# Ten instead of five first columns of q and k in fp32, the second five rounded on VectorE

## The chip, the cores and the metric

The kernel runs on one core of a Trainium2 chip. The metric is the device time of one execution in microseconds, the median of several runs. Profiles come from single executions of the same program; their "span" goes from the first to the last instruction and is a few microseconds shorter than the device time.

## The reference, cut to what matters

Four batches of channel attention are followed by a mixture of eight low-rank adapters with the two best chosen by gate.

```
B, N, C = (4, 6400, 256)
qn = q / (np.linalg.norm(q, axis=1, keepdims=True) + 1e-06)
kn = k / (np.linalg.norm(k, axis=1, keepdims=True) + 1e-06)
s = kn.transpose(0, 2, 1) @ qn / tau
a = np.exp(s - s.max(-1, keepdims=True))
a /= a.sum(-1, keepdims=True) + 1e-09
x = (v @ a).reshape(B * N, C)
...
z = x[mask] @ A[e]
delta[mask] += w[mask, k, None] * (z @ B[e])
...
return (x + delta).astype(np.float32)
```

The norms and the product of k and q run over the 6400 positions, so all of a batch's q and k has to be read before its attention matrix `a` (256 x 256) exists; only then can its v be worked on.

## The kernel before, in words

**Tiles.** The 6400 positions of a batch lie on 128 partitions with 50 "columns" each, and one column is 128 positions of 256 channels. A row of a column in DRAM is 1 KB of fp32. q and k of a batch are held in two halves of 25 columns (`QK`), v in five tiles of ten columns. In SBUF they are bf16: the loads issued by GpSimd (line 710, in the profile POOL) round fp32 to bf16 on the way. There are four `qk` tiles, so the load of a later batch's half waits until every reader of an earlier half is done.

**The work on q and k.** For each column `do_G` (line 753 for k with q, 757 for k with k, 761 for q with q) adds to an accumulator in PSUM. The diagonal of k with k and of q with q gives the norms. To spare TensorE, the table `OFF` takes some groups of five columns out of lines 757 and 761; for these, ScalarE squares the group (`do_sq`, line 776) and VectorE adds the squares up (`do_add`, line 783). The first group goes to a sum tile `ssq`, later groups through one single buffer `sq`, so square and add take turns. At the end of a batch `do_red` (789, 792) halves the sum down to 256 numbers, `do_n2p` (798) adds over the partitions on TensorE, `do_n2` (817) takes the diagonal, with ScalarE's copy of the accumulator (805), and reciprocal roots, exponentials and a transpose make the attention matrix. In batch 0 the groups taken out are 0, 1, 2, 3, 4, 6, 7 of k and 0, 2, 4, 5, 9 of q.

**The work on v.** Each tile of v is transposed on TensorE (`T`, 940), copied out of PSUM, multiplied with the attention and adapter weights (`ZL`, 964), gated on VectorE, and multiplied out (`Y`, 1067 and 1072); ScalarE and VectorE copy the outputs to the buffer `y` (920, 922), and SyncE stores them (1083).

**The order.** A planner in Python (`Plan.run`) works out a fixed order of instructions on every engine before the kernel is built, from estimated times. Some stores are held until a certain load has landed (`HOLD`).

**The opening.** Loads through GpSimd can round, loads through SyncE and ScalarE can't. The first five columns of q and k of batch 0 go the second way, as fp32, q issued by SyncE and k by ScalarE, ahead of everything else (`first_ahead`). They land in the first slot of the not yet used output buffer `y`. ScalarE rounds them into the `qk` tiles (`do_cast`, line 925), k first and then q, since the plan expects them so. `PARTS` cuts the rest of the first half: columns 5 to 16 and 17 to 24 are two more loads for each of q and k, issued by GpSimd. The adapter weights, 264 KB in three small loads, are issued by SyncE and ScalarE right behind the early columns and land in slot 1 of `y`; VectorE rounds them in `do_wts` (678, 681, 683). The last 16 partitions of columns 40 to 49 of batch 0 come by an indirect load (706).

The planner's steps and times are the same in both kernels.

Of the kernel before, what the change touches and what calls it, by code (L numbers as in the profile page):

```python
# [32 lines left out]
class Clock:  # L33


    WINDOW, FIRST, LOW, HIGH = 3.413, 0.31, 0.5, 0.8
# [249 lines left out]
def make_plan(B, order, ahead):  # L286
# [6 lines left out]
    for kind, b, i in order:  # L293
        if kind == "v":
# [3 lines left out]
            continue  # L298
        for c, n in PARTS.get((b, i), QK[i:i + 1]):
            for h in "qk":  # L300
# [3 lines left out]
    for h in "qk":  # L304
        p.add(("cast", h), {"ACT": 1.2}, [("load", h, 0, 0) + PARTS[0, 0][0]], 0)
    for b in range(B):

        for i, (c0, n) in enumerate(QK):
            for c in range(c0, c0 + n):
                deps = [k for k in p.steps if k[0] == "load" and k[2:4] == (b, i) and k[1] != "v"  # L310
                        and k[4] <= c < k[4] + k[5]]
                if (b, c) < (0, PARTS[0, 0][0][1]):
                    deps = [("cast", k[1]) for k in deps]
# [32 lines left out]
        if b == 0:  # L346
            p.add(("wts",), {"DVE": 2.12}, [("load", "k", 0, len(QK) - 1) + PARTS[0, len(QK) - 1][1]], -200)

# [118 lines left out]
        ('k', 2, 0), (2, 2): ('v', 1, 3), (2, 3): ('v', 2, 2), (3, 3): ('v', 2, 2)}  # L467

PARTS = {(0, 0): ((0, 5), (5, 12), (17, 8)), (0, 1): ((25, 17), (42, 8)), (3, 1): ((25, 17), (42, 8))}
REST, REST_AT, FULL, SIDE = (0, 1), 40, 112, 5  # L470
SLOTS = ((0, 4), (32, 34), (4, 6), (8, 12), (40, 42), (28, 32), (60, 62), (64, 68), (96, 98), (92, 96), (124, 126))
NO_WARM = {0, 1, 2, 3, 4, 5, 6, 7, 8, 9, 10, 11, 12, 24, 25, 26, 27, 28, 29}
# [105 lines left out]
def kernel(  # L578
# [11 lines left out]
    nc = tc.nc  # L590
# [15 lines left out]
    q_v = q.rearrange("b (p c) d -> b p c d", p=P)  # L606
    k_v = k.rearrange("b (p c) d -> b p c d", p=P)
# [10 lines left out]
    W = {}  # L618
# [3 lines left out]
    def y_slot(n):  # L622
        return Y[:, n * PC:(n + 1) * PC, :]
# [34 lines left out]
    held = {}  # L658

    def sb(s, kind, name, shape, dtype, part=""):  # L660

        if (kind, name, part) not in held:
            held[kind, name, part] = sbuf.tile(
                shape, dtype, tag=f"{kind}{at[kind, name]}{part}", name=f"{kind}{part}")
        return held[kind, name, part]
# [19 lines left out]
    def do_load(s, what, b, i, c, n):  # L685
        if what == "v":
            t, src = VS[:, at["v", (b, c // PC)] * PC:, :], v_v
        elif c + b:
            t = sb(s, "qk", (what, b, i), [P, max(n for _, n in QK), C], BF16)[:, c - QK[i][0]:, :]
            src = {"q": q_v, "k": k_v}[what]  # L690
        else:
            sb(s, "qk", (what, b, i), [P, max(n for _, n in QK), C], BF16)
            lo = "qk".index(what) * n
            W[what] = y_slot(0)[:, lo:lo + n, :]

            early.append((nc.sync if what == "q" else nc.scalar).dma_start(
                W[what], {"q": q_v, "k": k_v}[what][b, :, 0:n, :]))
            return
        r = P
        if what != "v" and (b, i) == REST:  # L700
            if c + n == NC:
                t, n, c, r = held["qk", (what, b, i), ""][:, REST_AT - QK[i][0]:, :], NC - REST_AT, REST_AT, FULL
            else:
                n = REST_AT - c
                for w in "qk" if what == "q" else "":
                    nc.gpsimd.indirect_dma_start(
                        W["side" + w].rearrange("p c d -> p (c d)"), None,
                        {"q": q, "k": k}[w].rearrange("b n d -> (b n d)").rearrange("(m w) -> m w", w=SIDE * C),
                        bass.IndirectOffsetOnAxis(ap=W["slots"], axis=0), bounds_check=B * N // SIDE - 1, oob_is_err=False)
        loaded[s.key] = nc.gpsimd.dma_start(t[0:r, 0:n, :], src[b, 0:r, c:c + n, :]).ins.name  # L710
# [211 lines left out]
            nc.vector.tensor_copy(out, in_)  # L922

    def do_cast(s, what):
        nc.scalar.copy(held["qk", (what, 0, 0), ""][:, 0:PARTS[0, 0][0][1], :], W[what])

    def do_warm(s, n):
        if n in NO_WARM:
# [149 lines left out]
    def do_store(s, b, i, c, n):  # L1078
# [3 lines left out]
        for rows in SHARES if (b, i) in SPLIT else (P,):  # L1082
            r = nc.sync.dma_start(out_v[b, p:p + rows, lo:lo + n, :], Y[p:p + rows, at_y:at_y + n, :])
            if (b, i) in HOLD and not p:
# [4 lines left out]


    do = dict(load=do_load, wts=do_wts, sq=do_sq, add=do_add, red=do_red, n2p=do_n2p, warm=do_warm, cast=do_cast, G=do_G, accs=do_accs, n2=do_n2, rsqrt=do_rsqrt, rq_ps=do_rq_ps, s=do_s,
              exp=do_exp, recip=do_recip, aT_ps=do_aT_ps, aT=do_aT, waA_ps=do_waA_ps, waA=do_waA,
              a=do_a, ZL=do_ZL, ZLe=do_ZLe, T=do_T, Te=do_Te, log=do_log, loge=do_loge, Z=do_Z, Ze=do_Ze, gzT=do_gzT,
# [56 lines left out]
```

## Time and profile before

| What | Value |
| --- | --- |
| median of 3 runs | 250.67 us (250.59 to 250.84) |
| the profiled execution | 250.69 us |
| its span | 245.0 us |
| TensorE busy | 213.6 us, 87% |
| VectorE busy | 185.4 us, 76% |
| ScalarE busy | 169.0 us, 69% |
| read and written in HBM | 79.90 MB and 26.21 MB, 433 GB/s over the span |
| GpSimd's loads (q0) | 38.67 MB as written in bf16 |
| hardware queues (q1 of SyncE, q10 of ScalarE) | 25.56 MB and 0.79 MB |

How to read it. PE is TensorE, PEld its weight loads, DVE VectorE, ACT ScalarE, POOL GpSimd, SP SyncE. A group's line has the source line, engine, operation, and "output<-input". In the timeline the first two numbers are the start and the length in microseconds, and brackets at the end hold the engine's idle time before the instruction and what ended it. A line of the waits says who waited for whom, microseconds in total, how often, and the longest. The chain of waits is followed back from the last instruction to what released it. A line of the DMA queues gives packets, megabytes and the packets' time as a share of sixteen DMA engines. q0's bytes are counted as written, bf16, so that it reads twice as many.

The opening in the before kernel, by view of the DMA issues: the early q was issued at 0.00 us and landed 4.9 us later, the early k at 0.12 with 5.9; GpSimd's first loads of q and k (12 columns) were issued at 1.44 and 2.09 and landed after 8.9 and 11.9 us.

### The profile page before, as it was taken

How to read it: one execution, taken by the hardware profiler on the slowest of the kernel's cores; microseconds unless marked ns; L12 is line 12 of the kernel's file. 1: busy time of each engine (PE TensorE's matmuls, PEld its weight loads, DVE VectorE, ACT ScalarE, POOL GpSimd, SP SyncE). 2: the span in 40 equal slices, each digit the busy share in tenths (PEclk: the TensorE clock that was granted, in tenths of full speed). 3: DMA queues.
4: the chain of work that ended last, by engine and by line, in shares of the span. 5: the costliest groups of instructions: out<-in, count | busy, mean ns of one | idle time of the engine just before them, and what ended most of it. 6: DMA issues, size and time to landing. Idle time of an engine off the chain costs nothing.

```text
span 245.0 us, 5349 instructions
## 1 busy us (share of the span) xinstructions
PE 213.6 (87%) x2203; PEld 178.1 (73%) x2024; DVE 185.4 (76%) x514; ACT 169.0 (69%) x316; POOL 27.6 (11%) x61
## 2 busy tenths in 40 slices
PE   0379099499898999999987999999999999999996
PEld 0257067158666998879877787999876799999985
DVE  1045578467869789999977889998989578788681
ACT  2944442274766769898796677999453599988885
POOL 7800200300020003000201003110000000000000
PEclk9999859769999999999999999999999999999999
DMA  8999999999999999999999999999999999999999
GB/s 276 214 214 217 210 231 205 214 222 214 215 216 218 220 209 217 221 215 206 243 290 258 318 295 206 214 221 223 306 213 301 352 381 283 309 407 438 422 416 417
DMA packets 8906, 65.36 MB, mean 267 GB/s; under 512 B 1201, under 2 KB 1585, under 8 KB 5170
## 3 DMA queue, kind: packets, MB, share of 16 engines
q0 software_dynamic: 5872, 38.67, 75.8%
q1 hardware_dynamic: 2674, 25.56, 25.2%
q10 hardware_dynamic: 336, 0.79, 0.9%
q8 instruction: 16, 0.26, 0.4%
q14 instruction: 8, 0.07, 0.1%
HBM read 79.90 MB, written 26.21 MB: 433 GB/s over the span
## 4 chain that ended last, share of the span: by engine, by line
DMA 39%; PE 37%; DVE 9%; issue 8%; ACT 6%; POOL 1%; POOLq 0%; ACTq 0%
DMA v<-in_v_dram 27%; PE Y_ps L1067 11%; DMA qk<-in_q_dram 7%; PE Y_ps L1072 5%; PE ZL_ps L964 5%; PE T_ps L940 5%; DMA qk<-in_k_dram 5%; DVE ssq L783 4%; PE acc L753 4%; PE gzT_ps L1054 3%; ACT sq L776 3%; DVE gz L1042 2%; PE acc L757 2%; ACT y L920 1%; POOL qk L710 1%
## 5 line engine op out<-in xcount | busy, mean ns | idle before, releaser
L753 PE MATMUL acc<-qk 128*128 128x256 bf16 (+1 forms) x400 | 77.5, 290 | 18.1 <-DMA qk<-in_k_dram 9.6
L783 DVE TENSOR_TENSOR ssq<-ssq,sq 128x1280 f32<-128x1280 f32 (+1 forms) x35 | 52.0, 1487 | 19.5 <-ACT sq L776 19.5
L753 PEld LDWEIGHTS <-qk 128*128 128x128 bf16 (+1 forms) x400 | 39.9, 105 | 31.0 <-DMA qk<-in_k_dram 10.3
L920 ACT COPY y<-Y_ps 128x512 f32<-128x512 f32 x87 | 50.7, 594 | 15.3 <-PE Y_ps L1072 12.8
L776 ACT ACTIVATE sq<-qk 128x1280 f32<-128x1280 bf16 (+1 forms) x35 | 44.8, 1280 | 23.2 <-DVE ssq L783 20.7
L1067 PE MATMUL Y_ps<-a_bf,vT 128*128 128x256 bf16 x400 | 60.0, 272 | 0.2 <-DVE zl L922 0.2
L1067 PEld LDWEIGHTS <-vT 128*128 128x128 bf16 x400 | 38.3, 98 | 5.2 <-issue 0.5
L1072 PE MATMUL Y_ps<-ball,gzT 128*128 128x256 bf16 x200 | 38.2, 273 | 0.0
L1042 DVE TENSOR_TENSOR gz<-zl,gatega 128x256 bf16<-128x256 f32 x95 | 35.4, 443 | 0.5
L757 PE MATMUL acc<-qk 128*128 128x128 bf16 (+1 forms) x170 | 32.6, 225 | 0.0
L940 PE MATMUL T_ps<-ident,v 128*128 128x128 f32 x200 | 25.8, 274 | 4.5 <-DMA v<-in_v_dram 4.2
L761 PE MATMUL acc<-qk 128*128 128x128 bf16 (+1 forms) x200 | 28.7, 227 | 0.0
L964 PE MATMUL ZL_ps<-waA_sb,vT 128*128 128x136 bf16 x380 | 26.3, 223 | 0.4 <-ACT y L920 0.3
L920 ACT COPY vT<-T_ps 128x512 f32<-128x512 f32 (+1 forms) x47 | 22.7, 546 | 4.6 <-PE T_ps L940 4.4
L940 PEld LDWEIGHTS T_ps<-ident,v 128*128 128x128 f32 x200 | 21.7, 141 | 5.8 <-issue 4.4
L964 PEld LDWEIGHTS <-vT 128*128 128x128 bf16 x380 | 23.8, 98 | 1.4 <-issue 0.4
L761 PEld LDWEIGHTS <-qk 128*128 128x128 bf16 (+1 forms) x200 | 19.1, 102 | 4.9
L920 ACT COPY zl<-ZL_ps 128x408 f32<-128x408 f32 (+1 forms) x50 | 19.9, 457 | 3.4 <-PE ZL_ps L964 3.4
L1054 PE MATMUL gzT_ps<-ident,gz 128*128 128x128 f32 x100 | 19.7, 280 | 2.0 <-DVE gz L1042 1.9
L1072 PEld LDWEIGHTS <-gzT 128*128 128x128 bf16 x200 | 19.5, 98 | 2.4 <-DVE gzT L922 0.2
L710 POOL DMA_DIRECT2D qk<-in_q_dram x11 | 6.2, 560 | 104.4 <-ACT y L920 40.2
L922 DVE COPY zl<-ZL_ps 128x272 f32<-128x272 f32 (+1 forms) x26 | 12.7, 497 | 6.9 <-PE ZL_ps L964 6.6
(91 smaller groups left out, 220.0 us busy)
## 6 DMA issues: line engine op xcount, KB each, us to landing
out_dram<-y SPq DMA_DIRECT2D x10, 1280.0 KB, 12.1
out_dram<-y SPq DMA_DIRECT2D x4, 2560.0 KB, 17.4
v<-in_v_dram POOLq DMA_DIRECT2D x14, 640.0 KB, 27.6
qk<-in_q_dram POOLq DMA_DIRECT2D x5, 1600.0 KB, 16.4
qk<-in_k_dram POOLq DMA_DIRECT2D x5, 1600.0 KB, 23.4
v<-in_v_dram POOLq DMA_DIRECT2D x3, 1280.0 KB, 28.6
out_dram<-y SPq DMA_DIRECT2D x3, 512.0 KB, 5.8
qk<-in_q_dram POOLq DMA_DIRECT2D x1, 1088.0 KB, 19.9
```

The lines of the kernel that those rows point to most:

```text
L753: nc.tensor.matmul(acc[ic][:, 0:256], kt[0:r, j, ic::CC], qt[0:r, j, :], start=c == 0, stop=False, skip_group_check=True)
L757: nc.tensor.matmul(acc[ic][:, 256:384], kt[0:r, j, ic::CC], kt[0:r, j, ic::CC], start=False, stop=False, skip_group_check=True)
L761: nc.tensor.matmul(acc[ic][:, 384:512], qt[0:r, j, ic * P:(ic + 1) * P], qt[0:r, j, ic * P:(ic + 1) * P], start=False, stop=c == NC - 1, s ...
L776: nc.scalar.activation(out[0:r, 0:n, :], t[0:r, j:j + n, :], ACT.Square)
L783: nc.vector.tensor_tensor(out=t, in0=t, in1=held["sq", (w, b, g), ""][0:r, 0:n, :], op=OP.add)
L920: nc.scalar.copy(out, in_)
L940: nc.tensor.matmul(ps[:, j, :], vt[:, c + j, :].bitcast(FP32), W["ident32"], is_transpose=True, start=(j == 0), stop=(j == n - 1))
L964: nc.tensor.matmul(ps[:, j, :], vT_of(b, i, c + j)[:, :, ic], st[b]["waA"][:, ic, :], start=(j == 0 and ic == 0), stop=(j == n - 1 and ic ...
L1042: nc.vector.tensor_tensor(out=pairs[:, h].rearrange("p c (e r) -> p c e r", e=E), in0=z[:, 2 * h:2 * h + 2, :].rearrange("p c (e r) -> p c ...
L1054: nc.tensor.matmul(ps[:, j, :], pairs[:, j * P:(j + 1) * P], W["ident32"], is_transpose=True, start=(j == 0), stop=(j == n // 2 - 1))
L1067: nc.tensor.matmul(ps[:, j, :], vT_of(b, i, c + j)[:, :, ic], st[b]["a"][:, ic, :], start=(j == 0 and ic == 0), stop=False, skip_group_che ...
L1072: nc.tensor.matmul(ps[:, j, :], pair[:, :, j], W["B"], start=False, stop=(j == 1), skip_group_check=True)
```

## The change

The early loads bring ten columns instead of five, in slot 0 of `y` for q and slot 3 for k. GpSimd's loads that the plan calls columns 5 to 16 now bring 10 to 16. ScalarE rounds the first five columns as before; VectorE rounds the next five, k and then q, right after ScalarE's instruction in the program.

```
+FIRST = 10
...
-            lo = "qk".index(what) * n
-            W[what] = y_slot(0)[:, lo:lo + n, :]
+            W[what] = y_slot(3 * "qk".index(what))
 
             early.append((nc.sync if what == "q" else nc.scalar).dma_start(
-                W[what], {"q": q_v, "k": k_v}[what][b, :, 0:n, :]))
+                W[what], {"q": q_v, "k": k_v}[what][b, :, 0:FIRST, :]))
             return
         r = P
+        if what != "v" and b == 0 and c < FIRST:
+            t, n, c = t[:, FIRST - c:, :], c + n - FIRST, FIRST
...
     def do_cast(s, what):
-        nc.scalar.copy(held["qk", (what, 0, 0), ""][:, 0:PARTS[0, 0][0][1], :], W[what])
+        n = PARTS[0, 0][0][1]
+        nc.scalar.copy(held["qk", (what, 0, 0), ""][:, 0:n, :], W[what][:, 0:n, :])
+        nc.vector.tensor_copy(held["qk", (what, 0, 0), ""][:, n:FIRST, :], W[what][:, n:FIRST, :])
```

## The prediction

> **What bounds the kernel now.** I read the page first, then the waits of TensorE, then the chain of waits in order of time, and last the timeline of the opening.
>
> ```profile
> span 245.0 us, 5349 instructions
> ...
> DMA  8999999999999999999999999999999999999999
> ...
> q0 software_dynamic: 5872, 38.67, 75.8%
> q1 hardware_dynamic: 2674, 25.56, 25.2%
> ```
>
> The DMA engines are busy in every slice but the first: the two large queues alone fill 101% of sixteen engines. So the time is that of the stream of bytes, plus a start and a tail. The median of the runs is 250.67 us; the profiled one took 250.69, so 5.7 us lie outside the span of 245.0 and everything below is reckoned inside the span.
>
> ```profile
> PE T_ps L940 <- DMA v<-in_v_dram: 4.2, 4, 2.5
> PE gzT_ps L1054 <- DVE gz L1042: 1.3, 2, 1.2
> ```
>
> These are TensorE's own waits between 50 and 135 us. It waits four times for v, the last time 2.49 us until 130.14. The chain of waits shows the same corner:
>
> ```profile
> 26.92 16.40 DMA qk<-in_q_dram
> ...
> 92.88 37.13 DMA v<-in_v_dram x2
> 130.14 2.38 PE T_ps L940 x20
> ```
>
> Before 130 us the stream of loads leads; from 130.14 the chain runs through TensorE, which is busy over 9.4 us in every 10 up to 240. So the end moves as the landing at 130.0 moves, unless something makes TensorE more than about 4.2 us late before that (its waits for v are its slack).
>
> The change acts in the opening, whose timeline on ScalarE is a serial chain:
>
> ```profile
> 6.03 2.42 ACT L925 CAST qk<-y 128x1280 bf16<-128x1280 f32 x2 [2.00 <-DMA y<-in_k_dram]
> 8.35 2.42 ACT L776 ACTIVATE ssq<-qk 128x1280 f32<-128x1280 bf16 x2
> 10.68 1.25 ACT L776 ACTIVATE sq<-qk 128x1280 f32<-128x1280 bf16 x1
> ...
> 14.04 1.27 ACT L776 ACTIVATE sq<-qk 128x1280 f32<-128x1280 bf16 x1 [2.11 <-DMA qk<-in_k_dram]
> ```
>
> After the two casts come two squares, then square and add take turns (one sq buffer): one turn is 2.83 us (14.04, 16.87, 19.70 ...). Squares run on without a data wait to 37.37.
>
> **Part 1: bytes move from POOL's queue to SP's and ACT's.** Ten columns of q and k instead of five, 1.31 MB of fp32 more, go by hardware queue; POOL's first two loads shrink from 12 columns to 7. Packet prices, from the DMA view by stretches: in 2 to 4 us, q10's 57 packets of 5 KB took 35.2% of 16 engines, 0.198 us each; in 12 to 14 us, q0's 68 packets of 6 KB took 100.7%, 0.474 us each. A row before costs 0.198 + 0.474 = 0.672. After it: one 10 KB packet, by q1's average on the page (25.2% of 245 x 16 for 25.56 MB) 0.396, and 3.5 KB of q0, 0.474 x 7/12 = 0.277: 0.673. Over 256 rows on 16 engines that is 16 x 0.001, nothing. POOL issues as many transfers as before (0.55 each), SP and ACT too, with as many rows. The stream is as long as it was.
>
> **Part 2: the gap at the start.** From 1.0 to 2.5 us q1 alone starts 63 packets that fill 98.5% of the engines: 0.375 us each instead of 0.198, together 63 x 0.177/16 = 0.70 us lost. If the loss is so much per packet or per byte, larger packets win nothing. If it is a supply of so many packets a microsecond, twice the bytes go through and up to 0.70 is won. No row tells these apart; as the records are long rather than few, I take 0.25 and keep 0 to 0.70.
>
> **Part 3: the early columns land later, the cast starts later.** q0 starts 16 packets between 4 and 6 us and 64 between 5.5 and 7.5, so it begins near 5.5. By then the half-microsecond stretches from 1.0 add up to 1.52 MB. Of 2.62 MB some 1.1 would be left, 2.7 us at 0.41 MB/us, and from 5.5 on POOL's packets take turns with them (0.28 beside 0.40 for each hardware queue), which adds 1.0 to 1.4. Data end near 9.3; before, the data of both ended near 5.0 to 5.3 and the cast began at 6.03. So the cast starts near 9.8 instead of 6.03. Bounds: 8.9 if POOL's packets keep out of the way, 13.5 if they all go first.
>
> Both loads keep one completion each, so the first five columns wait for all ten. Behind the cast on ScalarE stand the two squares, the first sq, and the chain of turns. From the cast to the first sq is 4.65 (10.68 - 6.03), one turn more is 2.83: the second sq starts at 9.8 + 7.48 = 17.3, not 14.04. The whole chain of squares is late by S = 3.3 us; bounds 2.3 and 6.9. Three things wait for it:
>
> (a) TensorE's first columns: 8.50 becomes 12.3, ending 2.29 later at 14.6. The wait for k that ended at 14.00 is gone, as columns 5 to 9 are already there, so it is 0.6 late. Its next wait, 6.40 us for k until 30.68, covers that; without cover it would cost 0.6.
>
> (b) POOL's next load of q, issued at 26.92 when a square ends. It becomes 30.2. The queue before it drains at about 35.4 (last landing 35.7), and from POOL's first issue at 1.44 to its first packet near 5.5 took 4.1. So it has 5.2 and needs at most 4.1. Covered, with 1.1 to spare.
>
> (c) The softmax of batch 0:
>
> ```profile
> 41.60 0.43 DVE L792 TENSOR_TENSOR ssqq<-ssq 128x256 f32<-128x256 f32 x1
> 42.59 0.29 DVE L817 SCALAR_TENSOR_TENSOR a_exp<-acc,ident 128x128 bf16<-128x128 f32 x1 [0.56 <-PE acc L757]
> ...
> 44.96 0.29 DVE L817 SCALAR_TENSOR_TENSOR a_exp<-acc,ident 128x128 bf16<-128x128 f32 x1 [1.86 <-ACT acc_sb L805]
> ```
>
> The last reduction ends at 42.03; VectorE then waits 0.56 for TensorE and 1.86 for ScalarE, which sits behind a load that lands at 43.34 in any case. So 2.4 of S is swallowed and 0.9 arrives in the softmax, at TensorE near 52. The four waits for v (4.2) swallow that by 130. Sum of part 3 at the end: 0, and 0.9 if those waits were not there.
>
> **Part 4: two more roundings on VectorE.** 1280 elements a partition from fp32 to bf16 in SBUF is not in the trace. From above: five times the 256-element row L683, 5 x 0.29 = 1.45. From below: the casts of L678 and L681, 256 elements in 0.29 and 16 in 0.175, so 0.49 ns an element, 0.80. I take 1.1 each, near the casts, 2.2 for both: 9.8 to 12.0. VectorE's first add would come at 15.7 and column 5 at 14.6, so they are hidden; were they needed at once, 2.2. Two extra waits on ScalarE or TensorE come with them, each for work done long before. Taking y's slot 3 costs nothing either: that buffer of outputs is first written at 64.40 us.
>
> The Trainium skill, "SBUF — State Buffer", section "SBUF: two separate sides", speaks against this part: an fp32 copy within SBUF on VectorE holds a port it shares with GpSimd, and GpSimd can't write descriptors meanwhile. No run here shows it; the nearest rows, POOL's issues at 91.84 to 93.42 with VectorE 9.45 of 10 us busy, took 0.53 to 0.54 as ever. By the page POOL's issues of 9.3 to 12.0 would slip by up to both roundings, an estimate of 2.2 us; by the rows by nothing.
>
> Even if POOL lost both roundings there, the load it issues at 10.33 would go out at 12.5, and the queue has work until 18.8.
>
> **Sum.** 0 (part 1) - 0.25 (part 2) + 0 + 0 = -0.25: 250.4 us, with 250.0 to 250.7 as its own range. A measurement of this kernel can't tell less than about 0.2%, 0.5 us, from no change, so most of this case counts as "same".
>
> **Rivals.**
> The opening is won whole: the larger packets fill the 0.70 us. For it: 0.375 against 0.198 us a packet while only one queue is served. Against it: the engines already read 98.5% busy. 250.67 - 0.70 = 249.97.
>
> Slower: the late cast makes POOL's load of 26.92 too late. Place: L710 behind the square of line 776. It decides once the cast starts after 9.8 + 1.1 = 10.9; from there each microsecond empties the queue for one, and the stream has no slack. A cast at 12.0 costs 1.1: 251.8. For it: small packets of SP and ACT dribbled behind POOL's until 9.3 (landings of 8.4 us after issue), so POOL may take more than its turn. Against: two hardware queues to one.
>
> Slower in another way: VectorE's roundings hold up POOL, or the 0.9 us in the softmax reach TensorE where it has no slack: some 0.6 to 0.9, 251.4. For it: TensorE is over 9.4 of 10 us busy from 80 to 120. Against: its 2.49 us wait at 130.
>
> The change does less than it says: PE's early start isn't made earlier by the five extra columns, since all ten have one completion; then 250.67 within the noise. This I count into the forecast.
>
> **How the numbers follow.** Forecast 0.52 (0.14 faster by over 0.2%, 0.38 same); opening won whole 0.20 (faster); POOL's load late 0.18 and the other slower case 0.10 (slower). Together faster 0.34, same 0.38, slower 0.28. The range goes from 249.7, a little beyond the whole opening, to 251.7, just short of the cast at 12.0: it leaves out some 0.05 below and 0.12 above.
>
> **What would show it.** The first cast near 9.8, the second sq near 17.3, POOL's next issue of q near 30.2, with no gap in the DMA row; the first softmax add of L817 under 1 us later; T_ps starting by 130.14 or up to 0.7 earlier, and the same distance from there to the end. In 1.0 to 2.5 us the bytes of q1 tell part 2: 0.32 MB as before, or up to 0.6. I am wrong if the landing at 130.0 moves later, if TensorE no longer waits for it, or if the rest after 130 grows.

## The result, and the profile after

The kernel after takes 251.57 us (median of 8 runs, 251.16 to 252.07), the kernel before beside it 250.66 (8 runs, 250.54 to 250.84). The ratio is 1.0035, with an interval of 1.0026 to 1.0044: slower by some 0.9 us, where 0.25 us less had been forecast. The profiled executions took 252.07 and 250.69; the first is the slowest of its eight, so the profiles lie 1.38 us apart where the medians lie 0.9 apart.

The page of the kernel after, its span and its queues (packets, MB, share of sixteen engines):

```profile
span 245.2 us, 5350 instructions
...
q0 software_dynamic: 5872, 38.01, 74.7%
q1 hardware_dynamic: 2630, 26.04, 25.7%
q10 hardware_dynamic: 336, 1.45, 1.5%
```

The span grew by 0.2 us, the execution by 1.38. So most of the loss is not in the span, which goes from the first to the last instruction. What lies around the span was taken as a constant 5.7 us in the prediction; it is 252.07 - 245.2 = 6.9 now. The windows of both kernels run on behind the last instruction (the last two columns are the share of the 16 DMA engines and GB/s). The kernel before:

```profile
245.00:247.00 2.00, 0.00 (x0) 0.00 (x0) 0.00 (x0) 0.00 (x0) 0.00 (x0) 1.00 1.03 422
247.00:249.00 2.00, 0.00 (x0) 0.00 (x0) 0.00 (x0) 0.00 (x0) 0.00 (x0) 0.67 0.75 299
```

And the kernel after:

```profile
245.00:247.00 2.00, 0.00 (x0) 0.00 (x0) 0.00 (x0) 0.00 (x0) 0.00 (x0) 1.00 1.03 422
247.00:249.00 2.00, 0.00 (x0) 0.00 (x0) 0.00 (x0) 0.00 (x0) 0.00 (x0) 0.79 0.94 377
249.00:251.00 2.00, 0.00 (x0) 0.00 (x0) 0.00 (x0) 0.00 (x0) 0.00 (x0) 0.50 0.12 45
```

Every engine but the DMA engines has stopped by 245.2, but the stores run on at full rate to about 248. Behind 247 the kernel before has 299 x 2 = 598 KB left to move, the kernel after (377 + 45) x 2 = 844 KB; the 246 KB between them are 0.6 us at the 422 GB/s of the row above. So the time is that of the stream of bytes to its very end, and the question is where the stream lost it. (In these rows a packet counts whole, with its bytes and its time, in the window in which it starts. So a share can be above 1, and a packet that is drawn out, that is, takes longer than its size needs, counts as busy all the while.) In the whole stretch from 28 to 40 us one window stands out. The kernel before:

```profile
32.00:33.00 1.00, 1.00 (x9) 0.45 (x3) 0.69 (x1) 0.28 (x1) 0.00 (x0) 0.50 1.28 264
33.00:34.00 1.00, 1.00 (x8) 0.56 (x4) 1.00 (x2) 0.16 (x1) 0.00 (x0) 0.50 1.01 212
```

The kernel after:

```profile
32.00:33.00 1.00, 1.00 (x9) 0.48 (x4) 0.00 (x1) 0.96 (x1) 0.40 (x1) 0.50 1.37 251
33.00:34.00 1.00, 1.00 (x14) 0.74 (x10) 0.66 (x1) 0.30 (x1) 0.00 (x0) 0.94 0.75 141
34.00:35.00 1.00, 1.00 (x15) 0.93 (x14) 0.83 (x1) 0.14 (x1) 0.00 (x0) 1.00 1.15 236
```

From 33 to 34 us the share, 0.97 or more in every other window of a microsecond from 30 to 36, reads 0.75, and the packets begun there bring 141 GB/s instead of 212. From 32 to 35 us the kernel after begins 628 KB where before begins 706: the 78 KB are some 0.36 us at 215 GB/s. The engines are not idle in that stretch: taken by the time that packets really run inside it, the window from 33 to 34 is filled to 0.98 in after and 1.03 in before. Packets are drawn out instead. "Dry" below means such a stretch, in which fewer bytes move. The 40 slices of the page are 6 us wide and read 9 in both kernels. Why there, the timelines of ScalarE and GpSimd tell (ScalarE before is shown in the prediction). ScalarE after:

```profile
10.43 2.42 ACT L928 CAST qk<-y 128x1280 bf16<-128x1280 f32 x2 [6.41 <-DMA y<-in_k_dram]
12.75 2.42 ACT L778 ACTIVATE ssq<-qk 128x1280 f32<-128x1280 bf16 x2
15.08 1.25 ACT L778 ACTIVATE sq<-qk 128x1280 f32<-128x1280 bf16 x1
17.89 1.27 ACT L778 ACTIVATE sq<-qk 128x1280 f32<-128x1280 bf16 x1 [1.56 <-DVE ssq L785]
```

GpSimd (POOL) before, and then after:

```profile
10.33 0.61 POOL L710 DMA_DIRECT2D qk<-in_q_dram  x1
10.90 0.61 POOL L710 DMA_DIRECT2D qk<-in_k_dram  x1
...
26.92 0.56 POOL L710 DMA_DIRECT2D qk<-in_q_dram  x1 [12.14 <-ACT sq L776]
```

```profile
10.33 1.05 POOL L712 DMA_DIRECT2D qk<-in_q_dram  x1
11.36 0.75 POOL L712 DMA_DIRECT2D qk<-in_k_dram  x1
...
30.77 0.56 POOL L712 DMA_DIRECT2D qk<-in_q_dram  x1 [16.06 <-ACT sq L778]
```

The cast starts at 10.43 and not at 6.03, the second sq at 17.89 and not at 14.04, and the square that frees the buffer of q lets POOL issue its load at 30.77 and not at 26.92, all late by 3.85 to 4.4 us. Behind it on POOL stand a load of k and one of v. By 33 about half of the sixteen engines had come to the end of what was queued before (the packet records are given further below).

VectorE after, the two roundings and the first add of the softmax:

```profile
10.43 1.57 DVE L929 CAST qk<-y 128x1280 bf16<-128x1280 f32 x2 [4.39 <-DMA y<-in_k_dram]
...
45.78 0.28 DVE L819 SCALAR_TENSOR_TENSOR a_exp<-acc,ident 128x128 bf16<-128x128 f32 x1
```

### The profile page after: what moved, and what is told of

It is laid out like the page before. It is cut to its first block, busy times and chain, and to the rows that moved or that the text cites. A ratio compares the mean times of both kernels' runs of the same rounds, so it can differ in the third digit from the quotient of the medians.

```text
span 245.2 us, 5350 instructions
## 1 busy us (share of the span) xinstructions
PE 211.4 (86%) x2203; PEld 176.0 (72%) x2024; DVE 186.6 (76%) x516; ACT 168.4 (69%) x316; POOL 28.2 (11%) x61
## 4 chain that ended last, share of the span: by engine, by line
PE 38%; DMA 31%; DVE 14%; ACT 9%; issue 8%; POOL 0%; POOLq 0%
DMA v<-in_v_dram 26%; PE Y_ps L1071 11%; DVE ssq L785 8%; PE Y_ps L1076 5%; PE ZL_ps L968 5%; PE T_ps L944 5%; DMA y<-in_k_dram 4%; ACT sq L778 4%; PE acc L755 4%; PE gzT_ps L1058 3%; DVE gz L1046 2%; PE acc L759 2%; ACT y L922 1%; ACT qk L928 1%; ACT ssq L778 1%
## 5 line engine op out<-in xcount | busy, mean ns | idle before, releaser
L755 PE MATMUL acc<-qk 128*128 128x256 bf16 (+1 forms) x400 | 74.4, 281 | 19.8 <-ACT qk L928 12.9
L755 PEld LDWEIGHTS <-qk 128*128 128x128 bf16 (+1 forms) x400 | 38.7, 102 | 31.9 <-ACT qk L928 11.7
L1046 DVE TENSOR_TENSOR gz<-zl,gatega 128x256 bf16<-128x256 f32 x95 | 35.4, 443 | 0.5
L759 PE MATMUL acc<-qk 128*128 128x128 bf16 (+1 forms) x170 | 32.9, 226 | 0.0
L763 PE MATMUL acc<-qk 128*128 128x128 bf16 (+1 forms) x200 | 27.6, 219 | 0.0
L763 PEld LDWEIGHTS <-qk 128*128 128x128 bf16 (+1 forms) x200 | 18.3, 98 | 4.1
```

Of the source, the lines that this page charges most:

```text
L755: nc.tensor.matmul(acc[ic][:, 0:256], kt[0:r, j, ic::CC], qt[0:r, j, :], start=c == 0, stop=False, skip_group_check=True)
L759: nc.tensor.matmul(acc[ic][:, 256:384], kt[0:r, j, ic::CC], kt[0:r, j, ic::CC], start=False, stop=False, skip_group_check=True)
L763: nc.tensor.matmul(acc[ic][:, 384:512], qt[0:r, j, ic * P:(ic + 1) * P], qt[0:r, j, ic * P:(ic + 1) * P], start=False, stop=c == NC - 1, s ...
L1046: nc.vector.tensor_tensor(out=pairs[:, h].rearrange("p c (e r) -> p c e r", e=E), in0=z[:, 2 * h:2 * h + 2, :].rearrange("p c (e r) -> p c ...
```

## The experiments

The expectations stand as they were written, and their theories go by letters. Those of the first sets (L, O, T, W, C, R, N and a first D, the larger share of the hardware queues or VectorE's roundings) are dropped later: most looked for the loss in the span, in TensorE's clock, in the softmax of batch 0 or in TensorE's wait for v at 130. The last two sets weigh another D, the DMA stream running dry behind a late issue, against E, the longer early transfers by themselves. A ratio is to the kernel before, run beside it, with its 95% interval.

**Both kernels again.** A copy of each.

> The kernel before once more, for the spans and clocks of its single runs, which the result of before lists only once (245.0 us, clock 0.972). Theory L (the late first cast costs time only where TensorE gets one more window at half clock): every run has a span of 245.0 to 245.2 and a clock of 0.972. Theory O (the 0.9 us arise outside the span): spans here are as spread as those of the changed kernel, 245.2 to 246.6, at the same times.

> The changed kernel once more: ratio near 1.0035. Both theories expect runs of two kinds, spans near 245.3 with clock 0.972 and near 246.5 with 0.965; the trace, if it is of the second kind, shows where the fifth half-rate window lies: theory L says between 43 and 56 us, in the softmax of batch 0; theory T says in the tail.

Measured: 250.91 us, ratio 0.9997 [0.9988, 1.0006], and 251.84, ratio 1.0039 [1.0026, 1.0052]. The loss stands. The spans of eleven runs of the copy of before went from 244.9 to 246.9 while the times stayed together, so a span says little about the time here.

**The single completion undone.** The kernel after, each early load cut in two:

```
-            early.append((nc.sync if what == "q" else nc.scalar).dma_start(
-                W[what], {"q": q_v, "k": k_v}[what][b, :, 0:FIRST, :]))
+            for lo, hi in ((0, n), (n, FIRST)):
+                early.append((nc.sync if what == "q" else nc.scalar).dma_start(
+                    W[what][:, lo:hi, :], {"q": q_v, "k": k_v}[what][b, :, lo:hi, :]))
```

> The changed kernel, with each early load cut into two transfers on the same queue, columns 0 to 4 and then 5 to 9, so that the first cast waits for five columns again; ten columns still go by hardware queue and VectorE still rounds five. Theory L: first cast near 6.2 to 7, second sq near 14 to 14.7, softmax as in the kernel before, time 250.5 to 250.8. Rival theory D (the larger share of the hardware queues, or VectorE's two roundings, cost the time): still 251.3 to 251.8.

Measured: 250.98 us, ratio 1.0001 [0.9992, 1.0010]. The same bytes, queues and roundings as after, and the loss is gone, as theory L asked and the first D did not. ScalarE and POOL of this kernel:

```profile
6.38 2.42 ACT L929 CAST qk<-y 128x1280 bf16<-128x1280 f32 x2 [2.01 <-DMA y<-in_k_dram]
```

```profile
27.13 0.56 POOL L713 DMA_DIRECT2D qk<-in_q_dram  x1 [12.15 <-ACT sq L779]
```

So neither the bytes on the hardware queues nor the roundings cost the time by themselves: it takes the wait of columns 0 to 4 for 5 to 9. The whole chain stands within 0.4 us of where it stood before.

**The cast late, nothing else.** The kernel before with idle squares on ScalarE ahead of the cast of k (five; then six and seven):

```
+        if what == "k":
+            for _ in range(DELAY):
+                nc.scalar.activation(y_slot(4)[:, 0:5, :].rearrange("p c (x d) -> p (c x) d", x=2),
+                                     W["ones"][:, None, :].to_broadcast([P, 10, P]), ACT.Square)
```

> The kernel before with five more ScalarE squares of 1280 elements (of ones, into a part of y that is not in use) ahead of its first cast, so that the cast of five columns starts near 10.1 instead of 6.03; loads and roundings as in the kernel before. Theory L: chain of squares late by 3.5 to 4, 251.3 to 251.8 us, spans of both kinds. Rival theory D: as the kernel before, 250.5 to 250.8.

> The kernel before with six ScalarE squares ahead of its first cast instead of five: first cast near 11.3, the chain of squares 1.2 us later than with five (which gave a ratio of 1.0011). Theory L (the end pays for the chain of squares beyond a slack): on a curve through five and seven, 251.5 to 252.2 where the kernel before takes 250.96. Rival R (a late first cast alone is nearly free, and the changed kernel loses by something that comes with the ten columns): 251.0 to 251.4.

> The same with seven squares: first cast near 12.5, chain of squares later by 2.4 us than with five. Theory L: each microsecond more costs nearly one, 252.5 to 253.3. Rival R: below 251.8.

Measured: cast at 10.16, 11.59 and 12.89; POOL's load of q issued at 30.49, 31.92 and 33.22; 251.14, 252.29 and 253.49 us; ratios 1.0011 [1.0002, 1.0021], 1.0064 [1.0051, 1.0077] and 1.0118 [1.0104, 1.0133]. With five squares the loss lies between what the two theories asked for. The windows of the kernel with seven:

```profile
32.00:33.00 1.00, 1.00 (x8) 0.49 (x4) 0.04 (x1) 0.93 (x1) 0.00 (x0) 0.50 0.62 123
33.00:34.00 1.00, 1.00 (x13) 0.74 (x10) 1.00 (x1) 0.00 (x0) 0.78 (x2) 0.92 0.43 87
34.00:35.00 1.00, 1.00 (x15) 0.93 (x13) 0.45 (x1) 0.52 (x1) 0.84 (x2) 1.00 1.46 207
35.00:36.00 1.00, 1.00 (x15) 0.93 (x13) 0.22 (x1) 0.75 (x1) 0.00 (x0) 1.00 0.30 51
```

The dry stretch of after, grown. From 31.92 to 33.22 the time rises by 0.0054 x 250.8 = 1.35 us for 1.30 us of lateness: about one for one, by two points with intervals of some 0.3 us either way. Carried back, that line meets no loss near an issue at 30.4.

**TensorE's clock, and a confounder.** Six kernels with 10 to 34 more matmuls. One is the kernel after with the fourth group of q's squares of batch 0 taken from ScalarE and VectorE and done by TensorE (10 matmuls), which makes the chain one turn shorter:

```
+ON_PE = {(0, 4, 'q')}
...
-        off = OFF if c < NC else ()
+        off = OFF - ON_PE if c < NC else ()
...
+        if (b, g, w) in ON_PE:
+            return
```

The others put idle matmuls ahead of the wait at 130 (ten), at 43 to 52 us (in after, in the shortened kernel and in before) or, as a control, at 21 to 23 us, in the wait that ends near 30 (ten). The control's edit, which also takes 6 out of `NO_WARM`:

```
+MORE = {6: 10}
...
+        ps = bank(s, ("warm", n), [P, 512], FP32)
+        for _ in range(MORE.get(n, 1)):
+            nc.tensor.matmul(ps, W["ident"], W["ident"][:, None, :].to_broadcast([P, 4, P]), start=True, stop=True)
```

> The changed kernel with one group (columns 20 to 24 of q, batch 0) taken from ScalarE and VectorE and given to TensorE (ten matmuls of line 763 more, in a stretch where TensorE waits for k later on): the chain of squares is one turn, 2.83 us, shorter, and everything else about the ten columns stays, the late landing and TensorE's late first column too. Theory L: the loss is gone, 250.6 to 251.2. Rival R: 251.6 to 252.0 as the changed kernel.

> The kernel before with ten idle matmuls of 512 columns put in front of the transpose of v that waits 2.5 us for its load at 130: TensorE then has no wait there long enough to lose its clock. In three of five traces of kernels with this wait no window at half clock followed, in two one did, 1.6 us. Theory W (this happens in the timed executions as in the profiled): faster than before by 0.5 to 1.0 us, spans near 245 alone. Rival: as before, 250.8 to 251.1.

> The changed kernel with idle matmuls put into TensorE's waits of batch 0's softmax (nine and six before the two sums over partitions, ten instead of five and ten instead of five behind them), so that its clock is not halved between 43 and 56 us. Theory C (the late chain of squares makes TensorE wait before its last columns, and the half clock that follows makes it 0.4 to 1.6 us late at 58 us, which the timed executions pay): 250.5 to 251.1 with the kernel before at 250.6. Rival O (something outside the softmax, in the opening): 251.5 to 251.9.

> The changed kernel with the shorter chain of squares (which took 251.82 although its softmax comes on time) and idle matmuls in the same places. Its trace without them had half clock from 43.9 to 54.1, three windows. Theory C: 250.4 to 251.0. Rival O: still 251.5 to 251.9.

> The kernel before with idle matmuls in the wait of 3.6 us before its softmax product and behind it. Theory C: TensorE earlier by up to 1 us at 58 us, the end faster by 0 to 0.5 us; not slower. Rival N (extra matmuls cost the timed executions 1 us wherever they stand, as ten of them at 128 us did): 251.5 or more.

> Control: the kernel before with ten idle matmuls in TensorE's wait of 6.4 us for k, at 24 us, where they take at most 4.3 us. Theory C: 250.5 to 250.8, as the kernel before. Rival N: 251.5 or more, as ten at 128 us gave 251.69.

Measured, in this order: 251.82 us, 1.0040 [1.0026, 1.0053]; 251.69, 1.0037 [1.0024, 1.0050]; 252.03, 1.0047 [1.0033, 1.0060]; 251.92, 1.0042 [1.0028, 1.0056]; 251.87, 1.0045 [1.0031, 1.0058]; 251.86, 1.0039 [1.0025, 1.0053]. By their medians all six are about 1 us slower than before, the three built from before too, and the control like the rest (single runs reach 250.67 in the first kernel and 250.98 in the second). So they tell nothing of the clock's worth, and no run was left that spoke for the theories of the clock: in these kernels more matmuls cost 1 us in all three places. The packet records name a suspect. Each of these kernels has 17 instruction fetches (q8, packets of 16 KB, 0.88 to 1.30 us on one engine each), all others have 16; in two of the six the seventeenth falls behind the span, so that their pages count 16.

**The same chain with the count kept.** The shortened kernel without the 11 idle matmuls at 43 to 52 us, and the kernel before without them:

```
-NO_WARM = {0, 1, 2, 3, 4, 5, 6, 7, 8, 9, 10, 11, 12, 24, 25, 26, 27, 28, 29}
+NO_WARM = {0, 1, 2, 3, 4, 5, 6, 7, 8, 9, 10, 11, 12, 13, 14, 15, 16, 17, 18, 19, 20, 21, 22, 23, 24, 25, 26, 27, 28, 29}
```

> The kernel after with the fourth group of q's squares of batch 0 moved to TensorE (10 matmuls more) as in the run of 251.82, and with the 11 idle matmuls at 43 to 52 us taken out, so that TensorE has about as many instructions as in before and 16 instruction fetches in place of 17. Theory D with the price of the seventeenth fetch (about 1.0 us): 250.5 to 250.9, ratio 0.998 to 1.001, POOL's load of q near 27.9. Theory E: 251.3 to 251.8. If the 11 idle matmuls had a worth of their own, the run below shows it.

> The kernel before without the 11 idle matmuls at 43 to 52 us; a control for the run above. Theory D: the end is set by the DMA stream, 250.5 to 250.9, ratio within 0.001 of 1, though TensorE's clock falls to half for some us after 45 and its span may grow. If TensorE's clock counted, 251.3 or more. A count of fetches below 16 would make it up to 1 us faster only if the last fetch delays the last store in before as well.

Measured: 250.80 us, 0.9996 [0.9987, 1.0005]; 250.95, 0.9999 [0.9990, 1.0008]. The page of the shortened kernel with them, and then without them:

```profile
q8 instruction: 17, 0.28, 0.4%
```

```profile
q8 instruction: 16, 0.26, 0.4%
```

Without the seventeenth fetch the shortened chain costs nothing against before, and removing the 11 matmuls from before moves nothing. That the fetch itself, and not something else that comes with the matmuls, is the 1.0 us is an inference from this pattern over eight kernels. The two losses don't add up either: the kernel after with idle matmuls has the late issue (30.28) and the seventeenth fetch, and pays 1.0047, not twice 1.004.

**POOL's load early in the kernel after.** The squares and adds of the fourth group of q of batch 0 are left out, so the norms of q in batch 0 lack these columns; no instruction is added:

```
+SKIP = {(0, 4, 'q')}
...
+        if (b, g, w) in SKIP:
+            return
```

> The kernel after without the squares of the fourth group of columns of q, batch 0 (their ACT square and DVE add are left out, so the norms of q in batch 0 lack these columns), and with no instruction added on TensorE. The chain of squares is one turn of 2.83 us shorter ahead of POOL's load of q, so that load should be issued near 27.9 us in place of 30.77. Theory D (the loss is the DMA stream running dry at 30 to 36 us because this load is issued late): no stall there, 250.4 to 250.8, ratio to before 0.998 to 1.000, with the opening's 0.25 us perhaps kept. Theory E (the longer early transfers leave one DMA engine behind up to the last store, whatever POOL does): 251.3 to 251.6, ratio 1.003 to 1.004. Both in part: near 251.1.

Measured: 250.84 us, 0.9995 [0.9986, 1.0004]. The cast is still late, at 10.54, and the chain is one turn shorter. POOL, and the window that was dry:

```profile
23.02 0.56 POOL L713 DMA_DIRECT2D qk<-in_q_dram  x1 [7.77 <-PE acc L756]
28.05 0.53 POOL L713 DMA_DIRECT2D qk<-in_k_dram  x1 [4.48 <-ACT sq L781]
```

```profile
33.00:34.00 1.00, 1.00 (x8) 0.69 (x6) 0.55 (x1) 0.42 (x1) 0.00 (x0) 0.50 1.01 210
```

The issue of q came earlier than expected, at 23.02, as the square that held it is gone; what is behind it went out at 28.05. The dry window is back at 210 GB/s, and the whole loss is gone with it. The long early loads and the late cast are still there, so theory E, that these loads cost the time whatever POOL does, is out.

**POOL's load late in the kernel before.** A memset on POOL ahead of one of its loads of q:

```
+        n_q[0] += what == "q"
+        if what == "q" and n_q[0] == 5:
+            nc.gpsimd.memset(t[0:r, 0:16, :], 0.0)
```

The first such run had 3 where 5 stands, all 15 columns of that load, and so met another load than the one meant:

> The kernel before with a POOL memset of the 17 columns of q put right ahead of the load that fills them (some 3.9 us by 1.16 us for five columns), so that only POOL's load of q and what is behind it on POOL are late: issue near 30.8 us in place of 26.92; early loads, cast and chain of squares stay. Theory D: the stream is dry for 0.6 to 0.9 us between 30 and 40 us and the run takes 251.4 to 252.0, ratio 1.003 to 1.005. Theory E: 250.6 to 250.9, ratio within 0.001 of 1, since the early loads are those of before.

```profile
10.33 3.31 POOL L713 MEMSET qk<- 128x3840 bf16 x1
13.93 0.58 POOL L714 DMA_DIRECT2D qk<-in_q_dram  x1 [0.30 <-POOL qk L713]
```

Measured: 251.01 us, 0.9997 [0.9988, 1.0006]. It says nothing of the question, but that POOL's load of 10.33 can go out 3.6 us later at no cost. Then the right one, with 16 and with 24 columns:

> The kernel before with a POOL memset of 16 columns of q right ahead of the load of q that POOL issues at 26.92 us. The memset of 15 columns ahead of an earlier load took 3.31 us, so this one takes some 3.5 us and with the 0.3 us between memset and load the issue stands near 30.8 us, as in the kernel after; early loads, cast and chain of squares are those of before. Theory D (the loss comes from this late issue alone): between 33 and 34 us the DMA share falls to about 0.75 as in after, and the run takes 251.3 to 251.9, ratio 1.002 to 1.005. Theory E (the longer early loads are needed as well): within 0.001 of 1, about 250.9.

> The same with 24 columns: a memset of some 5.3 us, issue near 32.6 us, 1.8 us later than in the run beside it. Theory D: each us beyond the point where the stream runs dry costs about one, so 1.5 to 2.2 us more than the run beside it, 252.9 to 253.9, ratio 1.008 to 1.012. Theory E: at most 251.5.

Measured: 250.92 us, 1.0003 [0.9994, 1.0012], and 252.73, 1.0068 [1.0054, 1.0081]. With 16 columns:

```profile
26.69 3.51 POOL L713 MEMSET qk<- 128x4096 bf16 x1 [11.90 <-ACT sq L780]
30.49 0.56 POOL L714 DMA_DIRECT2D qk<-in_q_dram  x1 [0.30 <-POOL qk L713]
```

```profile
33.00:34.00 1.00, 1.00 (x14) 0.85 (x11) 1.00 (x2) 0.16 (x1) 0.00 (x0) 0.97 0.88 182
34.00:35.00 1.00, 1.00 (x15) 0.93 (x13) 0.95 (x4) 1.00 (x1) 0.00 (x0) 1.00 1.24 259
```

Theory D asked for 0.5 to 1.0 us at this lateness and got 0.1: the stream dips to 182 and makes most of it up in the next window. With 24 columns the issue stands at 32.20 and the price is 1.7, on the line of the late casts (1.6 at 31.92, 3.0 at 33.22). So a late issue alone does cost what D says, but only from about 30.5 on.

The table puts the kernels with the late issue together. "Lost" comes from the packet records: each packet is charged with the before kernel's mean time per byte of its queue, and the running sum, divided by the sixteen engines, is set against before's; the column says how far the kernel falls back between 32 and 50 us.

```
kernel                   q issued   GB/s 33 to 34   lost, us   ratio to before
before                   26.92      212             0          1
before, POOL late        30.49      182             0.18       1.0003 [0.9994, 1.0012]
before, cast late (5)    30.49      212             0.20       1.0011 [1.0002, 1.0021]
after, again             30.34      179             0.33       1.0039 [1.0026, 1.0052]
after                    30.77      141             0.44       1.0035 [1.0026, 1.0044]
before, cast late (6)    31.92      228             0.93       1.0064 [1.0051, 1.0077]
before, POOL later       32.20      215             1.30       1.0068 [1.0054, 1.0081]
before, cast late (7)    33.22       87             1.90       1.0118 [1.0104, 1.0133]
```

(In the sixth and seventh row the dry windows are 32 to 33, with 138 and 169, and in the seventh also 34 to 35, with 97.) In both profiles of after the stream is 0.04 to 0.08 us ahead of before's at 32 us, loses 0.33 to 0.44 us by 50, and from there to 240 us nothing more. With the group left out and with the early loads split nothing is lost between 32 and 50. So this stretch is where the stream loses.

It is not the whole loss of time. By the line of the kernels built from before, an issue at 30.77 costs some 0.3 to 0.4 us and one at 30.34 next to nothing; the kernel after pays 0.9 to 1.0. The rest shows at the very end. Each engine closes its share of a store with a mark of four bytes; these are the last sixteen marks of each run:

```
kernel                    median mark   last mark   last - median
before                    248.54        249.02      0.5
before, again             248.78        249.59      0.8
after, early loads split  248.95        249.68      0.7
after, group left out     248.67        249.38      0.7
before, POOL late         248.86        249.39      0.5
before, cast late (6)     249.72        250.31      0.6
after                     249.22        250.40      1.2
after, again              248.90        250.34      1.4
```

In both profiles of after the last mark lies 0.4 to 0.9 us further behind the median than in the other kernels: one engine ends late. This goes away with the dry window, in the kernel with the group left out. So about half of the loss, 0.33 to 0.44 us, is the dry stretch, and the other half, as far as two profiles show it, is one engine that ends late. Why the dry window leaves one engine further behind in the kernel after than in the kernels built from before stays open; no run tells it.

## Why the prediction was wrong, point by point

**The bytes (part 1) and the opening (part 2)** went nearly as told. A 10-KB packet of q10 took 0.393 us and one of 3.5 KB of q0 0.288: 0.681 for a row, not 0.673, which over the 256 rows is 0.1 us more on sixteen engines. (The row of 68 packets in part 1 is that of 10 to 12 us; 12 to 14 has 101.) In 1.0 to 2.5 us the kernel after moved this:

```profile
1.00:1.50 0.50, 0.00 (x0) 0.00 (x0) 0.00 (x0) 0.00 (x0) 0.06 (x1) 1.00 1.68 287
1.50:2.00 0.50, 0.00 (x0) 0.00 (x0) 0.00 (x0) 0.00 (x0) 0.50 (x1) 1.00 0.56 164
2.00:2.50 0.50, 0.00 (x0) 0.00 (x0) 0.00 (x0) 0.33 (x1) 0.50 (x2) 1.00 0.77 307
```

These are 0.38 MB (the sum of the rates by half a microsecond) where before moved 225, 123 and 297, 0.32 MB: between the two ends named, nearer the lower. With packets charged as in the table above, the stream of after is 0.33 us ahead of before's at 8 us and 0.04 at 14. The copy of before stands 0.2 behind before at both, so the 0.25 that was taken is neither confirmed nor refuted. Whether anything of the gain lasts can't be told: the kernel after with its loss cured stands at 0.9995 [0.9986, 1.0004], or at 0.9996 for the shortened chain, both within what can be measured.

**The late cast (part 3)** was mis-sized by little: 10.43 (10.0 in the copy) for 9.8, the second sq 17.89 for 17.3, POOL's load of q 30.77 for 30.2. The chain is late by 3.85 us for 3.3, within the bounds of 2.3 and 6.9. By the prediction's own rule a cast at 10.43, before 10.9, was still covered.

**The step that failed is 3(b)**: "So it has 5.2 and needs at most 4.1. Covered, with 1.1 to spare." The 5.2 that it "has" was mis-sized; the "at most 4.1" that it needs held as a bound. The packet records of the late load of q (rows of 12.5 KB, eight for each engine) show both. Of each kernel, these are the first nine rows. In every kernel each of the nine begins before the first of them is done, so nine different engines move them:

```
kernel                 q issued   first rows begun   first rows done    one took
before                 26.92      32.49 to 32.85     33.45 to 33.81     0.96
before, POOL late      30.49      32.66 to 33.02     33.76 to 34.21     0.96 to 1.32
after                  30.77      32.63 to 33.36     34.02 to 35.20     1.07 to 1.86
before, cast late (6)  31.92      33.18 to 33.42     34.77 to 35.00     1.39 to 1.72
before, POOL later     32.20      33.46 to 33.62     34.98 to 35.61     1.48 to 2.15
before, cast late (7)  33.22      34.49 to 34.67     35.95 to 36.44     1.40 to 1.83
```

What it has: in before nine of the sixteen engines come free at 32.5 to 32.9, not at 35.4; that is when the last of them is done, some 2 us behind. From the issue at 30.77 to 32.63 there are 1.9 us (2.4 from the forecast 30.2), not 5.2. What it needs: with the issue at 31.92 to 33.22 the first rows begin 1.26 us behind it, but they are drawn out, and none is done before 2.7 to 2.9 us behind it; in the kernels of 30.49 and 30.77 the first is done 3.27 and 3.25 behind the issue. A first row that costs no time is done 0.96 behind 32.49, at 33.45. That puts the last issue that costs nothing, as an estimate, between 30.2 (3.25 before 33.45) and 30.7 (2.75 before); the line of the late casts met no loss at 30.4. In the prediction's own terms the point from which it decides, "once the cast starts after 10.9", lies at 9.9 to 10.4, an estimate with the 20.34 us from cast to issue in after. The rival with this mechanism was there, with 0.18. It is what happened, from a point 0.5 to 1.0 us earlier than worked out; its price of one microsecond for each covers about half of the loss, and the late engine at the end was in no rival. That 251.57 lies within the range of 249.7 to 251.7 says little for the sum: it lies in the part that was left open for this rival.

**The frame** failed too, "everything below is reckoned inside the span", with 5.7 us outside as a constant. The landing of v at 130 moved by 0.09 and the span by 0.2, so the signs named for a failure were nearly silent; the loss stands behind the last instruction, where the stores still run. In 14 of 20 profiled executions the device time is the last four-byte mark of a store plus 1.65 to 1.71 us; five of the other six are kernels with the seventeenth fetch. TensorE's chain from 130 on was the bound of the span, not of the time.

**The softmax (3c)** came late by 1.4 us instead of 0.9: VectorE begins the first step behind the four adds at 47.16 and not at 45.77. (The first of these adds is 3.2 us late, 45.78 for 42.59, where the sign asked for less than 1; before's wait of 1.86 us comes only behind it and took up that much.) On TensorE 0.4 was left at 55 us and nothing at 74, before the wait for v at 130 was reached. **TensorE's first columns (3a)** were covered as told.

**The roundings (part 4)** took 1.57 for both, 0.79 each, the bound from below (0.80), and hid as told. The Trainium skill's warning, "SBUF — State Buffer", section "SBUF: two separate sides", that such a copy keeps GpSimd from writing descriptors, shows in the trace: while the roundings run from 10.43 to 12.0, POOL's two issues take 1.05 and 0.75 where both took 0.61 before. In all eight profiles with roundings each rounding has an issue of POOL's that ends 0.12 us behind it, as if it had waited for it. The two lose 0.58 us in all, and not the 2.2 of the estimate from the page, as the roundings are shorter than taken and much of their time falls on the 0.61 that an issue takes anyway. The run that delayed the first of these issues by 3.6 us shows that this costs nothing.

**The other rivals.** The opening won whole (249.97) didn't come. That the softmax or the roundings reach TensorE late is excluded: the kernel with the split loads keeps the roundings and loses nothing, and TensorE's lateness is gone by 74 us.

## What to carry to other kernels

In a kernel whose DMA engines read 9 in every slice, the time can be that of the last store: look for lost time in windows of a microsecond, where a dry stretch shows, and past the end of the span. A load that gives ten columns one completion makes the first five wait for the last; two transfers kept the bytes on the same queue and cost nothing (1.0001). And when a queue is to cover a wait, reckon to the moment when its first engines run out (here 32.5 us), not to its last landing (35.7).

## What the runs showed of the hardware that had not been expected

Ten or more matmuls added on TensorE, at 21, at 43 to 52 or at 128 us, came with a loss of 1.0 us: with them the program has a seventeenth 16-KB instruction fetch, and taking out 11 others brings it back to sixteen and the time with it (ratio 1.0040 to 0.9996). That the fetch is the cause is inferred, as said above. Where this fetch falls at 243 to 245 us, the last mark of a store comes 1.2 to 1.7 us after the median one; where it falls at 250.5 or later, the last mark comes on time and the program ends 2.3 to 2.8 us after it instead of 1.7.

The span of one and the same kernel, before, went from 244.7 to 247.1 us while its times stayed within 0.4%. Two of its profiles show why the span moves: the copy has a window of half clock on TensorE from 130.0 to 133.4 us that the first lacks, and a span of 246.6 for 245.0. With the stores running on behind it, TensorE has about that much slack.
